# The first feed-forward matmul's last three groups by 26 products of half a batch in place of Strassen's 7, with their weight sums read back from DRAM

## The chip, the core and the metric

The kernel runs on one core of a Trainium2 chip. The core has a matmul engine (TensorE, PE in the profile; its weight loads are shown apart as PEld), three engines that work elementwise on tiles (VectorE = DVE, ScalarE = ACT, GpSimd = POOL) and SyncE (SP), which issues DMAs. Tiles lie in SBUF (128 partitions), matmul results in PSUM, eight banks of 512 float32 a partition. The metric is the device time of one execution in microseconds (us). Before the change it is 1294.29 us, the median of 3 runs (1294.07 to 1294.82).

## The reference

Attention with a root-mean-square norm on q and k, over 8 batches, 12 heads, 448 positions and 64 elements a head, and behind it a feed-forward block with SiLU over all 3584 = 8 x 448 tokens:

```python
q_n, k_n = rmsnorm(q, g_q), rmsnorm(k, g_k)
attn = softmax(scale * q_n @ k_n.T)            # per batch and head
x = (attn @ v).transpose(0, 2, 1, 3).reshape(3584, 768)
h = x @ w_in                                   # w_in  768 x 2048, float64
out = (h * sigmoid(h)) @ w_out                 # w_out 2048 x 768, float64
```

q, k, v are float32. The weights come as float64 and are rounded to float32 in the kernel.

## The kernel before

**Visits.** Four heads at a time make a *visit*, three visits a batch, 24 in all (c = 0 to 23, `NC`). A visit c does the scores and softmax of its heads and the product with v of the visit before (`visit`), with PE's share of attention some 13 us; `between(c)` then does the transposes and fills PE with matmuls of x @ w_in (`fill`). x @ w_in is made for two batches at a time, a *group* of 896 tokens, when their attention is done: group 0 in visits 6 to 11, group 1 in 12 to 17, group 2 in 18 to 23 (`GROUP` = 6), and group 3 alone, after visit 24, with no attention beside it. Then follows the output stage, h @ w_out, for all tokens (`quad`, QUADS = 7), by a deeper Strassen scheme in 192 columns.

**x @ w_in by Strassen.** x lies transposed in SBUF (feature by token, in `sets`). For two tiles of 128 hidden features and the group's two batches, a 2 x 2 scheme needs 7 products in place of 8, each of 3 steps (`HW`) of a 128x128 weight and 448 columns of x. `halves_in` goes through the eight pairs of feature tiles of a group, `part_in` names the operands of a pair, and the class `Seven` does the products: `two` makes products 1 and 2, `five` the others. A product ends in a PSUM bank; ACT copies products 1 and 5 to SBUF, DVE adds the others to what is there (`plus`, L912, one operand in PSUM), POOL adds twice between SBUF tiles (L984, L987). After the pair, ACT applies SiLU and SP writes 128x448 to `hidden` in DRAM (`activate`).

**The sums that Strassen needs.** Of w_in, in four chunks (`room.chunk(i)`, each of four feature tiles, with three sums beside it in `room.sums(i)`), they are made once by DVE (`sum_w_in`) during group 0 and stay in SBUF for all groups. Of x, four DVE operations for each of 3 rows of features make `sums_x` anew for each group (`sum_x`, L909 and L912).

**Rounding.** `Rounder.round` makes one piece of float32 weights of float64 ones: ACT takes two steps, DVE three (L126, L129, L133), POOL one (L137). w_in is rounded in the visits up to 11. w_out is rounded by `prepare_out` beside the products of group 3, two or more pieces at a time, 32 pieces of 128x384, with its Strassen sums by `right_sums` on DVE (L909, 16 of 128x768). It needs 4 chunks of room, which come free in turn: `ORDER` = 3, 0, 1, 2, chunk 3 in the first set of x (`sets[0]`), the others where w_in's chunk of the same number has been used.

**What sets the order.** Each engine works through its instructions in the order in which the program issues them, and waits for semaphores. `fill` issues W_in's matmuls a share at a time, with lists of small jobs (`others`, `prompt`) between them; `weights_in(c, half)` deals out the work on weights to the two halves of a visit. The PSUM banks are dealt by `bank(n)`: in visits one bank "mm" and, at times, one of the scores' ("sc"); once attention is over, two "mm" and six "alone". The other work on DVE in a visit is a merge of softmax parts (L803, 128x896), POOL's are the powers of the norm (L722, L503) and a scaling of q (L731).

## Time and profile before

One execution was profiled. Its span is 1294.6 us, beside the median of 1294.29 us of the three timed runs. The granted clock of PE shows 9, its full digit, in each of the 40 slices.

| engine | busy us | share of span | instructions |
|---|---|---|---|
| PE | 1283.5 | 99% | 7212 |
| PEld | 840.7 | 65% | 7212 |
| DVE | 971.4 | 75% | 1672 |
| ACT | 504.3 | 39% | 880 |
| POOL | 363.5 | 28% | 221 |

The stages, by time: attention alone and group 0 until 311 us, group 1 from 311 to 511, group 2 from 511 to 711, group 3 alone from 711 to 837.7, the output stage from there to the end. The page's slices show where the engines are full; a digit is the busy share of 1/40 of the span (32.4 us) in tenths, and the stage of group 3 are the slices 23 to 26:

```profile
PE   9999999999999999999999999999999999999998
DVE  6898878868666558666555886798978787878785
```

### The profile page before, as it was taken

The numbers are of one execution on the slowest core, as the hardware profiler recorded it, in microseconds if no ns is written. First come the engines' busy times: TensorE is split into PE (matmuls) and PEld (weight loads), VectorE is DVE, ScalarE is ACT, GpSimd is POOL, SyncE is SP. The second block draws the span as 40 slices with busy tenths as digits, with TensorE's granted clock in tenths as the row PEclk, the third lists the DMA queues.
The fourth block names the chain that finished last, engine by engine and source line by source line (L and its number), as shares of the span: only waits on it lengthen the run. The fifth ranks groups of instructions, "written<-read, shape, count | busy, mean of one in ns | idle before, by whom it ended". The sixth has DMA issues, their size and how long they took to land.

```text
span 1294.6 us, 19931 instructions
## 1 busy us (share of the span) xinstructions
PE 1283.5 (99%) x7212; PEld 840.7 (65%) x7212; DVE 971.4 (75%) x1672; ACT 504.3 (39%) x880; POOL 363.5 (28%) x221
## 2 busy tenths in 40 slices
PE   9999999999999999999999999999999999999998
PEld 4444454444444454444544555559999999999998
DVE  6898878868666558666555886798978787878785
ACT  7967666645555554554543344310001000000000
POOL 6765454543344344343311344400000000000000
PEclk9999999999999999999999999999999999999999
DMA  9675347434444444444411466312332313141411
GB/s 232 174 193 136 104 124 197 95 83 102 112 94 91 119 91 102 108 93 93 107 50 69 149 204 219 117 66 88 100 94 86 113 67 129 51 133 48 141 39 40
DMA packets 266160, 144.15 MB, mean 111 GB/s; under 512 B 203748, under 2 KB 249956, under 8 KB 266052
## 3 DMA queue, kind: packets, MB, share of 16 engines
q1 hardware_dynamic: 265424, 141.68, 39.8%
q8 instruction: 59, 0.97, 0.3%
q0 software_dynamic: 320, 0.90, 0.2%
q14 instruction: 49, 0.40, 0.1%
q10 hardware_dynamic: 308, 0.20, 0.1%
HBM read 95.36 MB, written 41.29 MB: 106 GB/s over the span
## 4 chain that ended last, share of the span: by engine, by line
PE 97%; DVE 1%; POOL 1%; issue 0%; ACT 0%; DMA 0%; SPq 0%; ACTq 0%; DVEq 0%; POOLq 0%
PE alone L1285 23%; PE mm L963 21%; PE sc L963 11%; PE av L789 10%; PE sc L752 10%; PE mm L1285 8%; PE alone L963 7%; PE alone L1323 2%; PE mm L832 2%; PE mm L1323 1%; PE sc L643 1%; PE sc L832 1%; PE sc L674 0%; DVE work L912 0%; POOL rms L503 0%
## 5 line engine op out<-in xcount | busy, mean ns | idle before, releaser
L757 ACT ACTIVATE work<-sc,rms 128x448 f32<-128x448 f32 x318 | 182.0, 635 | 98.0 <-PE sc L752 85.7
L752 PE MATMUL sc<-work 64*64 64x448 f32 x1344 | 169.4, 543 | 1.0 <-ACT work L653 0.6
L789 PE MATMUL av<-work,rows 64*64 64x448 f32 x1272 | 155.5, 540 | 1.2 <-DVE x L1514 0.9
L963 PE MATMUL mm<-x,W 128*128 128x448 f32 x366 | 149.1, 542 | 0.0
L963 PE MATMUL mm<-sums_x,W 128*128 128x448 f32 x348 | 142.4, 542 | 0.0
L803 DVE TENSOR_TENSOR work<-work 128x896 f32<-128x896 f32 (+1 forms) x110 | 118.3, 1105 | 28.6 <-PE av L789 28.1
L530 POOL DMA_DIRECT2D out_dram<-x x2 | 1.2, 592 | 443.5 <-DVE x L912 443.5
L503 POOL TENSOR_TENSOR rms<-rms,minus_half 128x14 f32<-128x14 f32 (+4 forms) x40 | 97.4, 2437 | 86.8 <-DVE rms L499 83.3
L963 PEld LDWEIGHTS mm<-x,W 128*128 128x128 f32 x366 | 68.5, 190 | 70.3 <-issue 64.8
L1285 PE MATMUL alone<-W,rows 128*128 128x192 f32 x610 | 113.0, 326 | 0.0
L963 PEld LDWEIGHTS mm<-sums_x,W 128*128 128x128 f32 x348 | 65.1, 190 | 68.1 <-issue 62.5
L789 PEld LDWEIGHTS av<-work,rows 64*64 64x64 f32 x1272 | 65.9, 132 | 62.8 <-issue 19.3
L752 PEld LDWEIGHTS sc<-work 64*64 64x64 f32 x1344 | 60.4, 132 | 63.3 <-ACT work L757 25.3
L1285 PEld LDWEIGHTS alone<-W,rows 128*128 128x128 f32 x610 | 101.4, 190 | 0.0
L963 PE MATMUL sc<-x,W 128*128 128x448 f32 x246 | 99.6, 541 | 0.0
L984 POOL TENSOR_TENSOR stage<-parts,stage 128x448 f32<-128x448 f32 x31 | 39.8, 1285 | 169.2 <-ACT stage L983 168.9
L722 POOL TENSOR_TENSOR rms<-rms,minus_half 128x28 f32<-128x28 f32 x15 | 72.6, 4842 | 48.9 <-DVE rms L719 47.8
L963 PEld LDWEIGHTS sc<-x,W 128*128 128x128 f32 x246 | 46.4, 190 | 47.0 <-issue 46.7
L1285 PE MATMUL alone<-W,work 128*128 128x192 f32 x382 | 72.2, 326 | 0.0
L1295 ACT COPY rows<-alone 128x192 f32<-128x192 f32 x33 | 10.5, 318 | 141.5 <-PE alone L1285 136.7
L1285 PEld LDWEIGHTS alone<-W,work 128*128 128x128 f32 x382 | 63.8, 190 | 0.0
L1116 ACT ACTIVATE stage<-stage 128x896 f32<-128x896 f32 x63 | 56.8, 945 | 17.1 <-DVE stage L912 16.9
(267 smaller groups left out, 2312.8 us busy)
## 6 DMA issues: line engine op xcount, KB each, us to landing
hidden<-stage SPq DMA_DIRECT2D x63, 448.0 KB, 2.9
work<-hidden SPq DMA_DIRECT2D x21, 1024.0 KB, 5.1
rows<-in_moe_w_out_dram SPq DMA_DIRECT2D x32, 384.0 KB, 3.7
W<-in_moe_w_in_dram SPq DMA_DIRECT2D x22, 512.0 KB, 5.3
x<-hidden SPq DMA_DIRECT2D x7, 1024.0 KB, 6.1
rows<-in_q_dram SPq DMA_DIRECT2D x120, 56.0 KB, 2.2
rows<-in_k_dram SPq DMA_DIRECT2D x120, 56.0 KB, 2.3
rows<-in_k_dram SPq DMA_DIRECT2D x60, 96.0 KB, 2.6
```

Of the source, the lines that this page charges most:

```text
L503: nc.gpsimd.tensor_tensor(out=t, in0=t, in1=half, op=ALU.pow)
L722: nc.gpsimd.tensor_tensor(out=f, in0=f, in1=minus_half.to_broadcast([P, n]), op=ALU.pow)
L752: nc.tensor.matmul(two[ds(half * D, D), h, 0:S], keys[rows, ts(half, D)], qT[rows, pair, :], start=True, stop=True,)
L757: nc.scalar.activation(left_weights(c)[:, h] if j == LEFT else weights(c, j)[:, i, h], two[:, h, 0:S], AF.Exp, scale=norm.column(c, i, h, j),)
L789: nc.tensor.matmul(sums[i][ds(h * D, D), :], v, w, start=(j == 0 and step == 1), stop=(j == LEFT - 1 and step == 1),)
L803: nc.vector.tensor_tensor(out=total, in0=total, in1=more, op=ALU.add)
L832: nc.tensor.matmul(t[ds(h * D + i * n, n), :], ones[:, which + i if which else 0], left_weights(c)[:, h] if which else w()[:, i, h], start ...
L963: nc.tensor.matmul(t, self.left(name, s), self.right(name, s), start=s == ends[0], stop=s == ends[1])
L984: nc.gpsimd.tensor_tensor(out=done[1, 2], in0=u2, in1=p5, op=ALU.add)
L1116: nc.scalar.activation(t, t, AF.Silu)
L1285: nc.tensor.matmul(t, x[:, i], y, start=i == ORDER[0], stop=i == ORDER[-1])
L1323: nc.tensor.matmul(o, a[:, 2 * i + m, t], right_one(name, i)[:, m], start=n == 0, stop=n == len(steps) - 1,)
```

## The change

Group 0 stays as it was. For groups 1 to 3, x @ w_in of one chunk (four feature tiles, 512 hidden features) is made by 26 products in place of 28: a scheme of 26 factors for a matrix of 4 by 2 blocks with one of 2 by 4. The blocks of x are half a batch, 224 columns; a product is 3 steps of a 128x128 weight and 224 columns. `FACTORS_LEFT` and `FACTORS_RIGHT` name each product's weight factor and x factor: numbers under 8 are blocks as they are, the others are sums (`LEFT_SUMS` 18 of weights, `RIGHT_SUMS` 18 of x). `AFTER` says which sums of products are made after which product and by which engine (last number: 0 is DVE, 1 POOL), 20 on DVE and 18 on POOL for a chunk.

- **Products** (`products_in`): two products of 224 columns share a PSUM bank; ACT copies the bank into two *blocks* of SBUF (33 blocks of 128x224 in the class `Blocks`, in what were sums of w_in and `stage`). `combine` then does the additions of `AFTER` between blocks, a bank later; when the two halves of a result are ready, ACT applies SiLU in place and SP writes it (`activate_some`).
- **Weight sums** (`form`): one operation of 128x384 each, once per chunk; chunks 0 and 1 on POOL in the visits 7 to 11, chunks 2 and 3 by DVE and POOL in turn in the visits 12 to 15 (`dealt`). `restore` first turns a block of weights that Strassen's sums had overwritten back into itself. `keep` writes each product's weights (128x384) to `lefts` in DRAM in the order of use.
- **Stream** (`Ring`): the weights of two products, 384 KB, are loaded by one DMA from `lefts` into a slot, as soon as a slot is free. There are 3 slots until chunk 2 has been formed (visit 13), 7 after that, 10 while group 3 runs alone, and for its last 13 pairs the 3 slots in the tail of `work`.
- **Sums of x** (`sum_right`): 18 operations of 128x672 a group in place of 12. Four are made a visit early on POOL (`EARLY_SUMS`), 7 on DVE and 7 on POOL in the visits 12 and 18 and ahead of group 3 (`LATE_SUMS`).
- **W_out**: `ORDER` is 0 to 3, the places are `sets[0]`, the room of chunk 3, `work`, the room of chunk 2; `prepare_out` is a flat list of small jobs, of which one is done ahead of each product. The regions of the output stage are dealt anew for that, by `carve` from named areas in place of `take`; what the output stage computes, and in which order, is unchanged.

On DVE, where group 3's products run, the rows read before (W: rooms of weights; stage and parts: results in SBUF; alone and mm: PSUM banks; L126 to L133: rounding of w_out; L909: its sums; L912: Strassen's additions):

```order
L133 SCALAR_TENSOR_TENSOR W<-rows,W 128x384
L909 TENSOR_TENSOR W<-W 128x768 x2
L909 TENSOR_TENSOR W<-W 128x2x384
L909 TENSOR_TENSOR W<-W 128x768
L912 TENSOR_TENSOR parts<-alone,parts 128x448
L912 TENSOR_TENSOR stage<-mm,stage 128x448
L912 TENSOR_TENSOR stage<-alone,parts 128x448
L126 TENSOR_SCALAR W<-W 128x384
L129 TENSOR_SCALAR W<-W 128x384
L133 SCALAR_TENSOR_TENSOR W<-rows,W 128x384
L912 TENSOR_TENSOR stage<-alone,stage 128x448
```

and now (L226 to L233 round, L1009 makes w_out's sums in x_172, which is `sets[0]`, and L1336 is `combine`; W and mixed hold its blocks):

```order
L1009 TENSOR_TENSOR x_172<-x_172 128x768
L226 TENSOR_SCALAR W<-W 128x384
L229 TENSOR_SCALAR W<-W 128x384
L233 SCALAR_TENSOR_TENSOR W<-rows,W 128x384
L1336 TENSOR_TENSOR W<-W 128x224
L1009 TENSOR_TENSOR x_172<-x_172 128x2x384
L1336 TENSOR_TENSOR mixed<-mixed 128x224 x2
L226 TENSOR_SCALAR W<-W 128x384
L229 TENSOR_SCALAR W<-W 128x384
L233 SCALAR_TENSOR_TENSOR W<-rows,W 128x384
L1009 TENSOR_TENSOR x_172<-x_172 128x768
L1336 TENSOR_TENSOR mixed<-mixed,W 128x224
```

The additions of products have half the columns, and none reads a PSUM bank: each has its operands and its result in SBUF.

On POOL at the same place before (L137: last step of rounding; L984 and L987: Strassen's additions):

```order
L137 TENSOR_TENSOR x_172<-x_172,rows 128x384 x2
L137 TENSOR_TENSOR W<-W,rows 128x384 x3
L984 TENSOR_TENSOR stage<-parts,stage 128x448
L137 TENSOR_TENSOR W<-W,rows 128x384
L987 TENSOR_TENSOR stage<-parts,stage 128x448
L137 TENSOR_TENSOR W<-W,rows 128x384 x3
L984 TENSOR_TENSOR stage<-parts,stage 128x448
L137 TENSOR_TENSOR W<-W,rows 128x384
```

and now (L237: last step of rounding; L1336: `combine`):

```order
L1336 TENSOR_TENSOR W<-W 128x224
L237 TENSOR_TENSOR W<-W,rows 128x384
L237 TENSOR_TENSOR W<-W,work 128x384
L1336 TENSOR_TENSOR mixed<-W 128x224
L237 TENSOR_TENSOR W<-W,rows 128x384
L237 TENSOR_TENSOR W<-W,work 128x384
L1336 TENSOR_TENSOR W<-W 128x224 x2
L1336 TENSOR_TENSOR W<-mixed 128x224 x2
L1336 TENSOR_TENSOR W<-W,mixed 128x224 x2
L1336 TENSOR_TENSOR mixed<-mixed 128x224
```

Between the steps of rounding there stand more and shorter additions.

On POOL, where visit 12 begins (group 1), the rows before (L722 and L503: powers of the norm; L731: scaling of q; L984 and L987: Strassen's additions of groups 0 and 1):

```order
L731 TENSOR_TENSOR rows<-rows,rms_61 128x896
L984 TENSOR_TENSOR stage<-parts,stage 128x448
L503 TENSOR_TENSOR rms_60<-rms_60,minus_half 128x14
L987 TENSOR_TENSOR stage<-parts,stage 128x448
L722 TENSOR_TENSOR rms_60<-rms_60,minus_half 128x28
L731 TENSOR_TENSOR rows<-rows,rms_60 128x896
```

and now, from the same scaling of q on (L822, L603 and L831 are the former L722, L503 and L731; L1255: sums of x; L1201: `restore`; L1217: weight sums; L1336: `combine`):

```order
L831 TENSOR_TENSOR rows<-rows,rms_61 128x896
L1255 TENSOR_TENSOR sums_x<-x_173 128x672 x2
L1201 TENSOR_TENSOR W<-W 128x6x128
L1217 TENSOR_TENSOR W<-W 128x384 x2
L1255 TENSOR_TENSOR sums_x<-x_173,sums_x 128x672
L603 TENSOR_TENSOR rms_60<-rms_60,minus_half 128x14
L1217 TENSOR_TENSOR W<-W 128x384
L1336 TENSOR_TENSOR W<-W 128x224
L1217 TENSOR_TENSOR W<-W 128x384
L1255 TENSOR_TENSOR sums_x<-x_173,W 128x672
L1336 TENSOR_TENSOR W<-W 128x224 x2
```

Sums of x and of weights stand ahead of, and between, the powers and additions.

The diff, cut to its core (the tables and the class `Blocks`, which hands out blocks singly or as two that one access reaches, are left out):

```diff
+AFTER = {
+    4: ((16, 100, "-", 104, 0),),
+    6: ((22, 103, "+", 106, 0), (1, 22, "-", 102, 1)),
...
+    def form(i, engines):
+        w = room.chunk(i)
+        s = room.sums(min(i, 3) if i < 2 else 3)
+        tiles = w.rearrange("p (r k f m) -> p r k f m", r=HW, k=2, f=room.CHUNK)
+        slots = [s[:, ds(n * K3, K3)] for n in range(6)]
+        held, order = {}, []
...
+        def restore():
+            halves = w.rearrange("p (c m r k) -> p c m r k", c=z.NW, m=2, r=2)[:, 0:HW]
+            nc.gpsimd.tensor_tensor(
+                out=halves[:, :, :, 1], in0=halves[:, :, :, 0], in1=halves[:, :, :, 1],
+                op=ALU.subtract,
...
+            engines[k % len(engines)].tensor_tensor(
+                out=source(name), in0=a, in1=b, op=ALU.subtract if op == "-" else ALU.add
+            )
+            if k < 4:
+                for n in (2 * k, 2 * k + 1):
+                    keep(n)
+            if order:
+                keep(order.pop())
...
+    def sum_right(group, engine, *names):
+        def one(name):
+            x, op, y = RIGHT_SUMS[name]
+            engine.tensor_tensor(
+                out=right_of(group, name), in0=right_of(group, x), in1=right_of(group, y),
+                op=ALU.subtract if op == "-" else ALU.add,
...
+        def more(self):
+            while self.n < (z.B // 2 - 1) * room.NC * PAIRS:
+                at = self.n % (room.NC * PAIRS)
+                if self.n >= self.last:
+                    self.free = [a for a in self.free if any(a is b for b in self.kept)]
+                if not self.free:
+                    return
+                i, t = divmod(at, PAIRS)
+                assert i in formed
+                slot = self.free.pop(0)
+                nc.sync.dma_start(slot, lefts[i, t])
+                self.ready.append(slot)
+                self.n += 1
...
+    def activate_some(now, most):
+        for _ in range(most):
+            if not silent or silent[0][0] > now:
+                return
+            _, f, b, two = silent.pop(0)
+            t = blocks.two(*two)
+            nc.scalar.activation(t, t, AF.Silu)
+            dst = hidden[f, :, ds(b * S, S)].rearrange("p (two s) -> p two s", two=2)
+            nc.sync.dma_start(dst, t)
+            blocks.release(*two)
...
+                (nc.gpsimd if engine else nc.vector).tensor_tensor(
+                    out=blocks[at[name]], in0=a, in1=b, op=ALU.subtract if op == "-" else ALU.add
+                )
...
+    def products_in(group, beside=lambda: None):
+        last = last_uses()
+        rows = list(carried)
+        carried.clear()
+        for i in range(room.NC):
+            at, places = {}, {}
+            for t in range(PAIRS):
+                slot = stream.next()
+                o = bank(S)
+                for h in range(2):
+                    beside()
+                    b = right_of(group, FACTORS_RIGHT[2 * t + h])
+                    for r in range(HW):
+                        nc.tensor.matmul(
+                            o[:, ts(h, T)], slot[:, ds(h * K3 + r * P, P)], b[:, r],
+                            start=r == 0, stop=r == HW - 1,
+                        )
+                        filler["ended"] = h == 1 and r == HW - 1
+                        yield T
+                filler["ended"] = False
+                now = clock[0] = clock[0] + 1
+                two = blocks.pair()
+                nc.scalar.copy(blocks.two(*two), o.rearrange("p (two s) -> p two s", two=2))
+                at[100 + 2 * t], at[101 + 2 * t] = two
+                stream.done(slot)
+                combine(now)
+                pending.append((at, group, i * room.CHUNK, (2 * t, 2 * t + 1), last, places))
+                if rows and t == 1:
+                    activate(rows)
+                activate_some(now, 2)
+                yield 0
...
-    ORDER = [3, 0, 1, 2]
+    ORDER = list(range(room.NC))
     n1 = room.size1
-    home = {i: (room.chunk(i), room.sums(i)) for i in ORDER[1:]}
-    home[3] = (sets[0][:, ds(0, n1)], sets[0][:, ds(n1, room.size2)])
+    full = n1 + room.size2
+    homes = [sets[0], None, work[:, 0:full], None]
+    home = {
+        i: (a[:, 0:n1], a[:, n1:full]) if a is not None else (room.chunk(j), room.sums(j))
+        for i, a, j in zip(ORDER, homes, (0, 3, 0, 2))
+    }
     bits = ring.bitcast(I32)
+    rows_end = own["rows"][:, 3 * z.DM + z.HALF :]
+    tail = work[:, full:]
...
+    def prepare_out():
+        sums = []
+        for i in ORDER:
+            sums.append([lambda i=i, k=k: right_sums(*chunk_out(i), steps=(k,)) for k in range(4)])
+        work = []
+        for i in ORDER:
+            more = [lambda: None] if not i else sums[i - 1]
+            if i == 2:
+                more = more + [lambda: fetch(0, 1, 1)]
+            for n in range(2 * room.CHUNK):
+                work += [rounder.open, rounder.round]
+                if n < len(more):
+                    work.append(more[n])
+            if i == ORDER[-1]:
+                work += sums[i]
+            while len(work) < (i + 1) * 2 * PAIRS:
+                work.append(lambda: None)
+        return iter(work)
...
+    both = (nc.vector, nc.gpsimd)
+    forms = [
+        form(i, engines) for i, engines in enumerate(((nc.gpsimd,), (nc.gpsimd,), both, both))
+    ]
+    forms[2].append(lambda: (stream.add(room.chunk(2)), stream.more()))
+    dealt = {3: (0, 4), 4: (0, 4), 5: (0, 4), 6: (0, 4), 7: (0, 3)}
+    dealt.update({8: (1, 5), 9: (1, 5), 10: (1, 5), 11: (1, 4)})
+    dealt.update({12: (2, 5), 13: (2, 5), 14: (2, 5), 15: (2, 5)})
+    dealt.update({16: (3, 5), 17: (3, 5), 18: (3, 5), 19: (3, 4)})
...
+    EARLY_SUMS = (11, 16, 12, 24)
+    LATE_SUMS = (8, 14, 22, 10, 15, 21, 17), (19, 9, 13), (18, 25, 23, 20)
...
+        elif c > GROUP and c % GROUP == 0:
+            columns = len(FACTORS_LEFT) * HW * T * room.NC
+            begin(products_in(last_two(c)), columns, 2 * GROUP, T, 2 * HW)
...
+        if c > GROUP and c % GROUP == 0:
+            vector, pool = (
+                sum_right(last_two(c), engine, *names)
+                for engine, names in zip((nc.vector, nc.gpsimd), LATE_SUMS)
+            )
+            run_all(vector[0:2])
+            late = vector[2:6] + late
+            late[2:2] = pool[0:1]
+            late[4:4] = pool[1:2]
+            late += pool[2:] + vector[6:]
...
-    for i in range(HW):
-        sum_x(group, i)
-    for m in range(2):
-        rows = [staged() for _ in range(2)]
-        begun[m] = rows, part_in(group, m, rows)
-        run(begun[m][1].two())
-    run(halves_in(group, range(HF), prepare_out, begun))
+    for engine, names in zip((nc.gpsimd, nc.vector, nc.gpsimd), (LATE_SUMS[i] for i in (1, 0, 2))):
+        run_all(sum_right(group, engine, *names))
+    stream.add(tail[:, 0 : 3 * 2 * K3])
+    stream.kept, stream.last = stream.free[-3:], ((z.B // 2 - 1) * room.NC - 1) * PAIRS
+    asides = prepare_out()
+    run(products_in(group, lambda: next(asides, lambda: None)()))
+    settle()
+    for at in ((0, 0), (0, 1)):
+        fetch(0, *at)
```

287 lines of the change are left out of this document (229 added, 58 removed), and 15 rows, old and new, of tables (AFTER, LEFT_SUMS, RIGHT_SUMS).

## The prediction

> **What bounds the kernel now.** I read the page's busy line and its chain by engine first.
>
> ```profile
> span 1294.6 us, 19931 instructions
> PE 1283.5 (99%) x7212; PEld 840.7 (65%) x7212; DVE 971.4 (75%) x1672; ACT 504.3 (39%) x880; POOL 363.5 (28%) x221
> PE 97%; DVE 1%; POOL 1%; issue 0%; ACT 0%; DMA 0%; SPq 0%; ACTq 0%; DVEq 0%; POOLq 0%
> ```
>
> TensorE is the bound: the chain lies 97% on it. So fewer matmul columns are worth their full time as long as nothing else becomes late. The span of this execution, 1294.6 us, stands 0.3 us above the median of the runs, 1294.29; I work from the span and take 0.3 off at the end.
>
> Next the windows view: two stages that the change rewrites, the second group's first half and the last group, which runs without attention (columns: stretch, length, busy PE, PEld, DVE, ACT, POOL, clock, DMA share, GB/s).
>
> ```profile
> 311.00:411.00 100.00, 99.98 (x548) 49.76 (x548) 66.03 (x89) 52.63 (x82) 40.85 (x18) 1.00 0.43 100
> 711.00:838.00 127.00, 127.00 (x342) 64.32 (x339) 99.28 (x163) 50.55 (x94) 51.76 (x47) 1.00 0.55 178
> ```
>
> In the last group DVE (99 us) and POOL (52 us) add up to more than the 127 us. That matters if the two can't work at once, so I looked for pairs that overlap in the timelines of both engines.
>
> ```profile
> 272.83 1.13 POOL L984 TENSOR_TENSOR stage<-parts,stage 128x448 f32<-128x448 f32 x1 [3.00 <-ACT stage L983]
> 388.77 1.91 POOL L987 TENSOR_TENSOR stage<-parts,stage 128x448 f32<-128x448 f32 x1 [6.28 <-DVE parts L912]
> 388.61 1.07 DVE L803 TENSOR_TENSOR work<-work 128x896 f32<-128x896 f32 x1
> 389.70 0.62 DVE L912 TENSOR_TENSOR stage<-sc,stage 128x448 f32<-128x448 f32 x1
> 259.35 1.91 POOL L987 TENSOR_TENSOR stage<-parts,stage 128x448 f32<-128x448 f32 x1 [0.18 <-DVE parts L912]
> 260.19 1.89 DVE L912 TENSOR_TENSOR W<-W 128x768 f32<-128x768 f32 x1
> 310.94 4.79 POOL L722 TENSOR_TENSOR rms<-rms,minus_half 128x28 f32<-128x28 f32 x1 [2.90 <-DVE rms L719]
> 314.56 0.62 DVE L909 TENSOR_TENSOR sums_x<-x,sums_x 128x448 f32<-128x448 f32 x1
> ```
>
> A POOL add of 448 columns takes 1.13 us alone, but 1.91 when a DVE add of two SBUF tiles (L803, from 388.61) is under way. A DVE add of two SBUF tiles that starts inside a POOL add (260.19, inside 259.35 to 261.26) takes 1.89, and its group below has a mean of 0.99: it waited out POOL's 1.07. A DVE add with one operand in PSUM (389.70, sc) ends inside the POOL add at its usual 0.62. So POOL's tile operations and DVE's operations on SBUF operands alone exclude each other; I call that the **port**. POOL's power on rms (L722, 310.94 to 315.73) is not part of it: DVE's add at 314.56 keeps its 0.62.
>
> **TensorE: what goes.** The chain gives back-to-back pitches for three widths.
>
> ```profile
> 711.18 2.45 PE mm L963 x6
> 713.63 6.76 PE alone L963 x18
> 837.66 5.16 PE mm L1323 x16
> 842.82 15.48 PE alone L1323 x48
> 880.24 3.90 PE alone L1285 x24
> ```
>
> 448 columns: 6.76/18 = 375.6 ns; 384: 15.48/48 = 322.5; 192: 3.90/24 = 162.5. The last two give 0.833 ns a column and 2.5 ns for each record, and 448 lies on that line, so 224 columns take 189.2 ns. A group before is 8 x 7 products x 3 steps at two records each, 336 x 375.7 = 126.2 us (711.18 to 837.66 is 126.5). After, it is 4 chunks x 26 products x 3 x 2 = 624 records x 189.2 = 118.1. That is **8.2 us a group, 24.5 us for three**; visits 12 to 23 get 1.4 us each shorter. No trace row has 224 columns: from below it can't beat 186.7 ns (0.833 x 224), which is 1.6 us more a group; from above it can't exceed the 322.5 of the 384.
>
> [...]
>
> **The port in the last group: what comes.** Prices first.
>
> ```profile
> L803 DVE TENSOR_TENSOR work<-work 128x896 f32<-128x896 f32 x78 | 84.3, 1114 | 28.1 <-PE av L789 28.1
> L909 DVE TENSOR_TENSOR W<-W 128x768 f32<-128x768 f32 x24 | 23.0, 992 | 2.7 <-POOL W L137 2.7
> L912 DVE TENSOR_TENSOR work<-work,x 128x384 f32<-128x384 f32 x28 | 15.5, 555 | 0.5
> 842.25 3.68 DVE L909 TENSOR_TENSOR W<-W 128x192 f32<-128x192 f32 x12
> 779.37 1.00 POOL L137 TENSOR_TENSOR W<-W,rows 128x384 int32<-128x384 int32 x1 [2.08 <-DVE W L133]
> 781.75 0.99 POOL L137 TENSOR_TENSOR W<-W,rows 128x384 int32<-128x384 int32 x1 [1.38 <-DVE W L133]
> 133.03 1.28 POOL L137 TENSOR_TENSOR W<-W 128x512 int32<-128x512 int32 x1 [1.56 <-DVE W L133]
> ```
>
> POOL: 384 columns 0.99, 448 1.13, 512 1.28, so 2.3 ns a column: 224 takes 0.615 us, 672 1.66. DVE: twelve adds of 192 in 3.68, 0.307 each; 32 columns more at 1.14 ns (768 against 384) make 0.34 for 224, and 672 takes 0.8. One rounded piece of W_out costs 2.37 us of the port (POOL's adds at 779.37 and 781.75: three DVE steps of 1.38 together, then POOL's 0.99, never side by side). In the last group after the change:
> - combinations (AFTER: per chunk 20 on DVE, 18 on POOL, every operand in SBUF): 80 x 0.34 = 27 and 72 x 0.615 = 44. Before, DVE's 40 adds read PSUM and cost the port nothing; POOL's 16 cost 18.
> - rounding, unchanged: 32 x 2.37 = 76. W_out's sums, unchanged: 16 x 0.9 = 14.
> - sums of x: 7 on DVE, 7 on POOL, 5.5 + 11.6 = 17. Before: 12 on DVE, 6.5.
>
> Sum 178 us, against 115 before (18 + 76 + 14 + 6.5), which fitted into 126. How much of the sum is really spent shows in the busiest stretch of before:
>
> ```profile
> 723.23 0.35 DVE L126 TENSOR_SCALAR x<-x 128x384 f32<-128x384 f32 x1
> 732.35 0.56 DVE L133 SCALAR_TENSOR_TENSOR x<-rows,x 128x384 int32<-128x384 int32 x1
> 724.74 1.00 POOL L137 TENSOR_TENSOR x<-x,rows 128x384 int32<-128x384 int32 x1 [19.13 <-DVE x L133]
> 730.70 1.00 POOL L137 TENSOR_TENSOR x<-x,rows 128x384 int32<-128x384 int32 x1 [0.98 <-DVE x L133]
> ```
>
> From 723.23 to 732.91, 9.7 us, stand four DVE roundings and five POOL adds (three of 384, two of 448 between the two quoted): by my prices 4 x 1.38 + 3 x 0.99 + 2 x 1.13 = 10.8. So 0.9 of the sum: **161 us**, more than TensorE's 118. Bounds: 118 if all overlapped (each engine alone has under 92), 179 if nothing does. I take 161, nearest to that stretch. TensorE can't run away from it: its products end in 8 banks, which ACT empties into blocks that the combinations free, and the output's first product needs W_out's last sum.
>
> ```profile
> 712.32 0.62 DVE L909 TENSOR_TENSOR sums_x<-x 128x448 f32<-128x448 f32 x1
> 836.04 2.69 DVE L909 TENSOR_TENSOR W<-W 128x768 f32<-128x768 f32 x3 [0.89 <-POOL W L137]
> ```
>
> Before, the port's work runs from 712.3 to 838.7 and the output stage starts at 837.7.
>
> **Visits 12 and 18** carry the sums of x, and 12 and 13 the weight sums of chunk 2. A visit:
>
> ```profile
> 344.78 0.16 DVE L765 COPY av<-minus_half 128x1 f32<-128x1 f32 x1 [0.69 <-PE av L789]
> 377.97 0.16 DVE L765 COPY av<-minus_half 128x1 f32<-128x1 f32 x1 [0.67 <-PE av L789]
> L731 POOL TENSOR_TENSOR rows<-rows,rms 128x896 f32<-128x896 f32 x12 | 21.0, 1748 | 0.9
> ```
>
> 33.2 us, 31.8 after. Port in visit 12: POOL 7 x 1.66 (x) + 4 x 0.99 and a restore of 768 at 1.9 (weights) + 12 x 0.615 + 1.75 (L731) = 26.6; DVE 4.6 x 1.1 (L803) + 7 x 0.8 + 5 x 0.55 + 13 x 0.34 = 17.8. Together 44, so 13 over; visit 13 has 26 and catches up. Visit 18, without weight sums: 36, 4 over. Of these 17 us between none and all reach TensorE; I take **7**, since 13 us of the next visit are attention and leave the port room.
>
> [...]
>
> **Hidden edits.** The weights now come from DRAM: 384 KB a pair of products, which TensorE uses for 12 x 189.2 = 2.27 us.
>
> ```profile
> rows<-in_moe_w_out_dram SPq DMA_DIRECT2D x32, 384.0 KB, 3.7
> 335.41 3.98 SPq L255 DMA_DIRECT2D rows<-in_k_dram  x8
> ```
>
> The ring has three slots in visits 12 and 13 and for the last 13 pairs: a load has two pairs, 4.5 us, and takes 3.7 by the row of the same size. I cost it at nothing; cover is gone when SP is busy with eight loads of k (3.98 us), which would cost 3.2 us each time. ACT gains 13 copies a chunk and stays under 60%. The first group's POOL sums (36 in five visits) lie in its idle time. W_out's new places and the output stage move no work. Three 1 MB fetches now start when the products end, about 10 us ahead of need: nothing.
>
> **Sum.** Groups two and three: -16.4 + 7 = -9.4, so the last group's port work starts at 702.9 and ends at 702.9 + 161 = 863.9. The output starts 1.5 us ahead of that end (the last combinations follow W_out's sum), at 862.4 in place of 837.7: +24.7. 1294.6 + 24.7 - 0.3 = 1319, which I round to **1320**.
>
> **Rivals.**
> - DVE and POOL fit into each other's gaps at this small size, and TensorE stays the bound. Then 1294.3 - 24.5 + 7 = **1277**, faster. For it: each engine alone has time; against it: rows 260.19 and 388.77. It decides below a port time of 136 us (837.7 + 1.5 - 702.9), where the result turns from slower to faster.
> - Port time between 136 and 150: 1294 to 1308, about the same to slower.
> - The weight stream is late as well: SP stands behind k's loads twice in visits 12 and 13 and its waits for POOL's sums come on top, 4 x 3.2 = 13 us on 1320, **1333**.
> - The change doesn't do what it says: 224 columns at more than 202 ns (126.2/624) save nothing. The records' own mean, 326 ns at 192 columns unpipelined, would be its extreme; the pitch rows speak against it. Some 1345.
>
> **How the numbers follow.** Forecast 0.58; overlap (1277) 0.20; between 0.12; late stream 0.08; no saving 0.02. The range reaches from the overlap's 1276 to 1338 (port 179). Faster by over 0.2%, about what a measurement of this kernel can tell from no change: the overlap and a fifth of the between, 0.22; within 0.2%: 0.05; slower: 0.73. On the slower side alone the range is 1300 to 1338.
>
> **What would show it.** Right: in the last group gaps of TensorE that end on ACT or on DVE's and POOL's adds, DVE and POOL adds well over 0.34 and 0.615 us in the mean, that group some 160 us long. Wrong: TensorE without gaps there and L1371 at 189 ns, or its waits ending on loads of lefts.

## The result, and the profile after

The changed kernel takes 1433.39 us, the median of 4 runs (1431.76 to 1438.17), beside 1294.18 (1293.99 to 1294.82, 4 runs) for the kernel before: 1.108 times as long (95% interval 1.106 to 1.110), 139 us slower. The page's first lines, and of its 40 slices those of TensorE and its granted clock:

```profile
span 1431.5 us, 22959 instructions
PE 1302.4 (91%) x8076; PEld 1018.8 (71%) x8076; DVE 1080.7 (75%) x1795; ACT 561.8 (39%) x1036; POOL 604.5 (42%) x480
PE   9999989997758799898999799488999999999997
PEclk9999999998979899999999999799999999999999
```

TensorE is no longer full, and in four of the slices in which it isn't (10, 12, 14 and 26) its granted clock shows 8, 7, 8 and 7 in place of 9. To see in which stage, I cut the span at the visits (DVE's copy of av<-minus_half stands at the head of each visit from 7 on) and at the output's first matmul: the visits 7 to 11, 12 to 15, 16 to 23, group 3 and the output stage. Before:

```profile
149.70:311.30 161.60, 161.60 (x907) 80.13 (x903) 125.89 (x172) 96.43 (x153) 70.92 (x40) 1.00 0.50 124
311.30:444.50 133.20, 133.16 (x724) 66.15 (x720) 86.34 (x116) 71.48 (x111) 52.34 (x23) 1.00 0.44 104
444.50:710.00 265.50, 265.37 (x1424) 130.08 (x1416) 168.23 (x223) 133.30 (x208) 90.71 (x42) 1.00 0.35 87
710.00:837.70 127.70, 127.50 (x345) 64.35 (x346) 99.12 (x163) 50.61 (x95) 51.76 (x47) 1.00 0.55 178
837.70:1294.60 456.90, 450.74 (x2648) 433.50 (x2646) 365.21 (x806) 39.86 (x112) 3.38 (x5) 1.00 0.26 85
```

and after:

```profile
149.30:330.80 181.50, 166.90 (x903) 79.86 (x895) 135.56 (x170) 96.55 (x153) 118.48 (x81) 0.98 0.63 168
330.80:522.00 191.20, 146.01 (x918) 110.61 (x920) 108.28 (x152) 81.70 (x140) 104.95 (x80) 0.87 0.67 193
522.00:801.20 279.20, 259.58 (x1808) 202.40 (x1800) 208.71 (x278) 159.21 (x279) 170.91 (x136) 0.98 0.69 187
801.20:964.00 162.80, 131.33 (x633) 125.16 (x634) 131.00 (x193) 69.14 (x143) 103.53 (x106) 0.90 0.70 238
964.00:1431.50 467.50, 453.67 (x2649) 434.58 (x2647) 371.07 (x813) 42.79 (x119) 9.88 (x14) 0.99 0.28 89
```

The columns are stretch, length, busy PE, PEld, DVE, ACT and POOL, clock, DMA share and GB/s. Length less busy PE is TensorE's idle time. The saving of matmul time is 8.2 us a group, so 5.5 us in four visits and 10.9 in eight; what busy PE has above its time before less this saving is time in which matmuls ran slowly, most of it at half clock, as is shown below.

| stage | before | after | saved | idle more | slow matmuls |
|---|---|---|---|---|---|
| visits 7 to 11 | 161.6 | 181.5 | 0 | 14.6 | 5.3 |
| visits 12 to 15 | 133.2 | 191.2 | 5.5 | 45.2 | 18.3 |
| visits 16 to 23 | 265.5 | 279.2 | 10.9 | 19.5 | 5.1 |
| group 3 | 127.7 | 162.8 | 8.2 | 31.3 | 12.0 |
| output stage | 456.9 | 467.5 | 0 | 7.7 | 2.9 |

So 24.6 us were saved, and 118 us of waits and 44 us of slow matmuls came. The saving itself is there. In TensorE's timeline, in group 3, twelve matmuls of 224 columns follow each other in 2.27 us, 189.2 ns each:

```profile
809.78 2.43 PE L1371 MATMUL alone<-x,W 128*128 128x224 f32 x12
812.05 2.43 PE L1371 MATMUL alone<-W 128*128 128x224 f32 x12
814.32 2.43 PE L1371 MATMUL mm<-x,W 128*128 128x224 f32 x12
...
370.61 6.34 PE L1371 MATMUL mm<-sums_x,W 128*128 128x224 f32 x24 [2.55 <-DMA W<-lefts]
...
896.35 1.37 PE L1371 MATMUL alone<-sums_x,W 128*128 128x224 f32 x6 [2.12 <-ACT work L204]
...
920.73 2.58 PE L1371 MATMUL alone<-W,work 128*128 128x224 f32 x6 [14.42 <-DMA work<-lefts]
923.10 2.45 PE L1371 MATMUL alone<-x,work 128*128 128x224 f32 x6
925.34 1.99 PE L1371 MATMUL mm<-x,work 128*128 128x224 f32 x6
927.17 1.30 PE L1371 MATMUL mm<-W,work 128*128 128x224 f32 x6
```

The last rows show the slow matmuls: after an idle time of 14.42 us, six take 2.37 us from start to start (920.73 to 923.10), twice their 1.14, and it takes 6 us until they are back. After 2.12 us of idle time nothing of it is seen; after 2.55 it is (24 in 6.34 us, where 24 at 189.2 ns take 4.5). In this trace every wait from 3.7 us on has it, and none under 2 us. The trace's record of the granted clock has 17 stretches at half clock up to the last matmul, each of 3.41 us or two, three or five times that. The length of a wait alone doesn't tell whether one comes: waits of 2.02, 2.23, 2.29, 2.55 and 3.07 us brought the half clock, and 2.12 and 3.38 us didn't. The 17 stretches are 109 us long, and TensorE was busy in 72 us of them; half of that, 36 us, is the clock's part of the 44. The other 8 us are not placed.

TensorE's longest waits in all:

```profile
PE mm L1371 <- DMA W<-lefts: 27.3, 9, 6.5
PE alone L1371 <- DMA work<-lefts: 24.4, 3, 14.4
PE mm L1371 <- DVE W L1336: 8.9, 1, 8.9
```

(us in total, times, longest.) The weight stream leads, with nearly half of the 118 us. Where its loads were, SP's timeline tells; first visit 12, then group 3:

```profile
345.49 3.98 SPq L355 DMA_DIRECT2D rows<-in_q_dram  x8
349.59 0.40 SPq L1285 DMA_DIRECT2D W<-lefts  x1
350.10 1.09 SPq L1104 DMA_DIRECT2D hidden<-mixed  x2
351.24 5.05 SPq L1197 DMA_DIRECT2D lefts<-W  x6
356.39 0.51 SPq L1285 DMA_DIRECT2D W<-lefts  x1
...
801.25 20.15 SPq L188 DMA_DIRECT2D rows<-in_moe_w_out_dram  x4
821.50 1.32 SPq L1285 DMA_DIRECT2D work<-lefts  x3
...
909.34 7.56 SPq L188 DMA_DIRECT2D rows<-in_moe_w_out_dram  x3
916.95 0.42 SPq L1285 DMA_DIRECT2D work<-lefts  x1
```

A load of the stream (L1285) stands behind eight loads of q, behind six writes of weight sums (L1197, 0.84 us each in the mean), or behind loads of w_out (L188) that wait for a buffer which rounding has yet to free: 801.25 to 821.4. SP's own waits in group 3 begin with these two (us in total, times, longest; L233 is DVE's last step of rounding):

```profile
SPq L188 <- DVE W L233: 27.7, 11, 4.6
SPq L188 <- DVE x L233: 27.4, 5, 18.1
```

### The profile page after: what moved, and what is told of

Read it like the earlier page. It is cut to its first block, busy times and chain, and to the rows that moved or that the text cites. A ratio compares the mean times of both kernels' runs of the same rounds, so it can differ in the third digit from the quotient of the medians.

```text
span 1431.5 us, 22959 instructions
## 1 busy us (share of the span) xinstructions
PE 1302.4 (91%) x8076; PEld 1018.8 (71%) x8076; DVE 1080.7 (75%) x1795; ACT 561.8 (39%) x1036; POOL 604.5 (42%) x480
## 5 line engine op out<-in xcount | busy, mean ns | idle before, releaser
L603 POOL TENSOR_TENSOR rms<-rms,minus_half 128x14 f32<-128x14 f32 (+4 forms) x40 | 101.1, 2530 | 71.8 <-DVE rms L599 68.7
L1629 PE MATMUL alone<-W,x 128*128 128x192 f32 x544 | 112.6, 326 | 0.0
L1629 PEld LDWEIGHTS alone<-W,x 128*128 128x128 f32 x544 | 92.5, 190 | 0.0
L1371 PE MATMUL mm<-W 128*128 128x224 f32 x306 | 72.2, 381 | 20.8 <-DMA W<-lefts 11.7
L822 POOL TENSOR_TENSOR rms<-rms,minus_half 128x28 f32<-128x28 f32 x15 | 72.4, 4825 | 40.4 <-DVE rms L819 39.6
L1371 PE MATMUL mm<-x,W 128*128 128x224 f32 x312 | 73.8, 375 | 15.2 <-DMA W<-lefts 13.0
L1371 PEld LDWEIGHTS mm<-W 128*128 128x128 f32 x306 | 62.2, 207 | 25.6 <-DVE W L1336 9.2
L1217 POOL TENSOR_TENSOR W<-W 128x384 f32<-128x384 f32 x54 | 60.5, 1136 | 25.9 <-DVE W L1217 18.1
L1639 ACT COPY sums_x<-alone 128x192 f32<-128x192 f32 x33 | 10.5, 318 | 141.0 <-PE alone L1629 141.0
L1065 PE MATMUL mm<-x,W 128*128 128x448 f32 x138 | 56.7, 546 | 3.4 <-ACT mixed L1076 1.7
L1643 ACT COPY x<-alone 128x192 f32<-128x192 f32 x34 | 10.9, 319 | 123.0 <-PE alone L1629 114.2
L1629 PE MATMUL alone<-W,work 128*128 128x192 f32 x244 | 57.2, 326 | 0.0
L1012 DVE TENSOR_TENSOR rows<-rows,x 128x192 f32<-128x192 f32 x72 | 25.7, 357 | 38.2 <-ACT x L1643 36.4
L575 DVE TENSOR_REDUCE rms<-rows 128x8 f32<-128x512 f32 (+2 forms) x50 | 31.9, 639 | 26.3 <-ACT rows L574 25.8
```

Of the source, the lines that this page charges most:

```text
L575: nc.vector.tensor_reduce(out=out, in_=t.rearrange("p (n d) -> p n d", n=n), axis=AX.X, op=ALU.add)
L603: nc.gpsimd.tensor_tensor(out=t, in0=t, in1=half, op=ALU.pow)
L822: nc.gpsimd.tensor_tensor(out=f, in0=f, in1=minus_half.to_broadcast([P, n]), op=ALU.pow)
L1012: nc.vector.tensor_tensor(out=out, in0=a, in1=b, op=ALU.add)
L1065: nc.tensor.matmul(t, self.left(name, s), self.right(name, s), start=s == ends[0], stop=s == ends[1])
L1217: engines[k % len(engines)].tensor_tensor(out=source(name), in0=a, in1=b, op=ALU.subtract if op == "-" else ALU.add)
```

## The experiments

Each kernel is the change with the edits shown; "as e2" and the like say whose edits it has besides. This table has the lengths of the stages, read as above; the output stage is counted to its last matmul. The column "whole" is the time of the run or, for the change, for e1 and e15, a median. A kernel that leaves work out can't be compared as a whole, only by stages. The lengths are those of one execution each, and they differ between runs whose edits don't concern the stage: 177.6 (e2) to 184.2 us (e9) for the visits 7 to 11, 191.0 to 193.6 (e9, e10) for 12 to 15, 278.7 to 282.2 (e10, e4) for 16 to 23, 160.3 to 162.9 (e3, e2) for group 3. So a difference of a few us between two runs, up to 6.6 in the visits 7 to 11, shows nothing by itself.

| run | whole | 7 to 11 | 12 to 15 | 16 to 23 | group 3 | output |
|---|---|---|---|---|---|---|
| before | 1294.2 | 161.6 | 133.2 | 265.5 | 127.5 | 450.9 |
| the change | 1433.4 | 181.5 | 191.2 | 279.2 | 162.8 | 459.2 |
| e1 ACT issues the loads | 1419.0 | 181.0 | 180.4 | 285.5 | 157.1 | 457.4 |
| e2 no sums, no writes, chunks 2, 3 | 1406.1 | 177.6 | 168.5 | 280.1 | 162.9 | 459.3 |
| e3 no writes, chunks 2, 3 | 1410.4 | 181.2 | 171.1 | 279.5 | 160.3 | 459.9 |
| e4 no sums, chunks 0, 1 | 1420.8 | 167.8 | 191.3 | 282.2 | 162.3 | 459.9 |
| e5 as e2, ACT issues the loads | 1384.1 | 180.2 | 149.6 | 284.7 | 156.7 | 457.3 |
| e6 as e2, seven slots | 1378.0 | 182.2 | 138.3 | 280.5 | 161.5 | 460.0 |
| e7 as e1, all product sums on DVE | 1404.5 | 179.0 | 189.3 | 276.8 | 150.6 | 453.0 |
| e8 no sums of x | 1398.6 | 175.8 | 188.9 | 265.4 | 150.9 | 459.9 |
| e9 less rounding of w_out | 1410.1 | 184.2 | 191.0 | 279.9 | 141.5 | 457.1 |
| e10 no loads for the last 13 pairs | 1421.6 | 181.1 | 193.6 | 278.7 | 135.5 | 476.1 |
| e11 every new addition on DVE | 1417.3 | 196.5 | 188.6 | 280.1 | 137.2 | 459.2 |
| e12 half the bytes of the stream | 1414.5 | 179.5 | 184.1 | 278.2 | 155.4 | 459.3 |
| e13 as e6, no sums of x | 1344.7 | 175.7 | 135.9 | 266.9 | 151.1 | 459.6 |
| e14 no sums, no writes, chunks 0, 1 | 1411.0 | 164.3 | 186.2 | 283.4 | 162.6 | 459.3 |
| e15 as e7, slots freed earlier | 1404.0 | 180.3 | 194.8 | 274.8 | 141.0 | 457.6 |

Two theories stood against each other: the *queue theory* (the stream's loads are issued late, behind the other work in SP's queue, as from 801.25 to 821.4 us, and three slots don't cover that) and the *port theory* of the prediction (DVE and POOL exclude each other on SBUF, as it read its rows 260.19 and 388.77, so sums and blocks are late).

**e1: the loads on ACT's queue.**

```diff
-                nc.sync.dma_start(slot, lefts[i, t])
+                nc.scalar.dma_start(slot, lefts[i, t])
```

> The loads of the weight stream are issued by ACT in place of SP; nothing else changes. Queue theory: TensorE's waits for lefts (24 us in the visits 12 to 14, 25 us beside group 3) come from loads that stand in SP's queue behind the writes of weight sums, the loads of q, k, v and the loads of w_out that wait for rounding. Then these waits go, with some 10 us of half-clock matmuls behind them: 1370 to 1395 in place of 1433, group 3 near 135 us. Port theory (DVE and POOL exclude each other, sums and blocks are late): other waits take their place, group 3 stays at 155 or more, 1420 to 1433.

1418.99 us, above the queue theory's range and just under the port's. The visits 12 to 15 gain 11 us and group 3 only 5.7: of the waits for lefts in group 3 9.7 us are left, but 14.6 us of waits for ACT's SiLU (behind blocks that DVE and POOL finish) came in their place. The visits 16 to 23 got 6.3 us longer.

**e2 and e3: chunks 2 and 3 without sums and writes, and without writes alone.**

```diff
+    forms[2], forms[3] = [lambda: None] * 19, [lambda: None] * 19   # e2
-                if name == n:
+                if name == n and i < 2:                              # e3
-                nc.sync.dma_start(slot, lefts[i, t])
+                nc.sync.dma_start(slot, lefts[i % 2, t])             # both
```

> The weight sums of chunks 2 and 3 and their writes to DRAM are left out (their products load the weights of chunks 0 and 1 instead). Both theories: the visits 12 to 15 (191 us now, 133 before the change) fall to about 130 us, the whole by some 60 us to 1375. If they stay above 150, the stream itself or the sums of x are to blame.

> The weight sums of chunks 2 and 3 are made, but not written to DRAM (their products load the weights of chunks 0 and 1). Queue theory: SP has 9 to 11 us less to issue in each of the visits 12 to 15, and nothing waits for a write: the four visits fall from 191 to 140 to 150 us. Port theory: the 36 additions are what costs; the four visits stay above 175 us.

Without the writes the four visits take 171.1 us, without writes and sums 168.5. So the 52 writes cost 20 us; the 2.6 of the 36 additions are within what runs differ by. The port theory, which said 175 or more without the writes, falls for this place. What it is in a write that costs, these runs don't separate. Beside SP's time, DVE stood idle in the four visits until a write had landed and the place of its sum could be used again:

```profile
DVE W L1217 <- DMA lefts<-W: 19.5, 6, 7.2
```

e3 takes away both, SP's work and this wait. But 168.5 is far above the 130 that both expected: visits 12 and 13 still take 46.6 and 57.6 us, 14 and 15 are down to 32.6 and 31.7. What the first two have alone is three slots and the late sums of x.

**e5 and e6: the same without SP, and with seven slots.** (e6 has SP issue the loads.)

```diff
+                nc.scalar.dma_start(slot, lefts[i % 2, t])           # e5
                 stream.add(room.sums(2))
+                stream.add(room.chunk(2))                            # e6
```

> The weight sums of chunks 2 and 3 and their writes are left out (their products load chunks 0 and 1), and ACT issues the stream's loads; three slots in the visits 12 and 13. Queue theory: with SP's queue out of the way the stream is on time, the visits 12 and 13 take 34 us each (46.6 and 57.6 with the loads on SP). Slot theory: a slot comes free two pairs, 4.5 us, ahead of its next use, and a load takes 4.6 us from issue to landing; the waits for lefts stay, at 40 us or more a visit.

> As the run without the sums of chunks 2 and 3, with SP issuing the loads, but with seven slots from visit 12 on in place of three. Slot theory: the visits 12 and 13 fall from 46.6 and 57.6 to 34 us each, since a load may be six pairs late. Queue theory: SP's eight loads of q or k (4 us) are covered by seven slots as well, so the same. If they stay above 40 us, neither slots nor SP's queue are it, but the sums of x on DVE and POOL.

The visits 12 to 15 in e2, e5 and e6 (columns as above):

```profile
327.15:495.63 168.48, 141.78 (x918) 110.89 (x920) 94.19 (x133) 81.30 (x140) 79.91 (x60) 0.90 0.59 162
327.45:477.09 149.64, 135.97 (x918) 102.84 (x920) 93.49 (x134) 81.84 (x140) 79.08 (x60) 0.96 0.69 183
329.44:467.77 138.33, 133.44 (x918) 103.40 (x920) 92.03 (x134) 81.17 (x140) 80.46 (x60) 0.96 0.73 199
```

With three slots and ACT's queue visits 12 and 13 take 42.0 and 43.0 us, with seven slots 34.6 and 39.5, and no wait for lefts is left in the four visits. Of the 30 us that four more slots bring (168.5 to 138.3), 19 come by the queue alone (149.6). So it is slots and queue together: three slots were too few for loads that were issued late. (All three runs are without weight sums and writes; whether seven slots would have covered the writes too, no run shows.)

**e12: half the bytes.**

```diff
-                nc.sync.dma_start(slot, lefts[i, t])
+                nc.sync.dma_start(slot[:, 0:K3], lefts[i, t, :, 0:K3])
-                            o[:, ts(h, T)], slot[:, ds(h * K3 + r * P, P)], b[:, r],
+                            o[:, ts(h, T)], slot[:, ds(r * P, P)], b[:, r],
```

> Each load of the weight stream brings 192 KB in place of 384 (both products of a pair use the first one's weights); number, order and slots stay. Transfer theory: the 4.6 to 5.5 us from issue to landing are transfer time on busy DMA engines and fall to some 3.5; with three slots and 4.5 us that ends the waits for lefts where SP isn't late: the visits 12 and 13 fall from 112 to about 90, group 3 by 10. Queue theory: the issue itself is late, not the transfer; the visits and group 3 change by less than 5 us.

Landing fell as the transfer theory said. The DMA view of the stretch from 330 to 490 us, the change and then e12 (count, KB each, median us from issue to landing):

```profile
W<-lefts SPq DMA_DIRECT2D x31, 384.0 KB, 4.2
```

```profile
W<-lefts SPq DMA_DIRECT2D x29, 192.0 KB, 3.2
```

One microsecond less, and visits 12 and 13 fell only from 112.0 to 107.8 us, where the transfer theory said 90; group 3 fell by 7.4. So in the visits late issue weighed more than the transfer.

**e4, e14 and e11: the weight sums of chunks 0 and 1 in the visits 7 to 11.** e4 leaves the sums out, e14 the writes too (its products load other data from DRAM); e11 moves all additions that the change brought, these among them, from POOL to DVE; as in e15, ACT issues the loads and a slot is freed by its own pair, so e11 is to be compared with e15.

```diff
+            if i > 1:                                                # e4
                 engines[k % len(engines)].tensor_tensor(
...
+    forms[0], forms[1] = [lambda: None] * 19, [lambda: None] * 19   # e14
...
-        form(i, engines) for i, engines in enumerate(((nc.gpsimd,), (nc.gpsimd,), both, both))
+        form(i, engines) for i, engines in enumerate(((nc.vector,),) * 4)    # e11
...
-            engine.tensor_tensor(
+            nc.vector.tensor_tensor(                                 # e11
```

> The 36 weight sums of chunks 0 and 1 on POOL (visits 7 to 11) are left out; their writes to DRAM stay. Port theory: the five visits, 181.5 us now against 161.6 before the change, come back to 162 to 166 us. Queue theory (52 writes on SP): they stay above 176 us.

> The weight sums of chunks 0 and 1 and their writes are left out (their products load other data of the same size from DRAM). If the writes are the 6 us that stayed without the sums, the visits 7 to 11 take 161 to 164 us (167.8 without the sums alone, 161.6 before the change). Rival, the sums of x of visit 11 and other moves: 166 or more.

> All additions on POOL that the change brought are made by DVE (products' sums, sums of x, weight sums of all chunks), ACT issues the loads, and a slot is handed on as soon as its own products are done. Port theory: POOL's tile operations cost the port 1.8 times DVE's; the visits 7 to 11 come from 181 to 172 us, 16 to 23 from 277 to 268, group 3 from 151 to 138, the whole from 1404 to about 1375. Rival, DVE alone becomes the bound in the visits: 7 to 11 above 181.

181.5 us became 167.8 without the sums, 13.7 of the 19.9 us that were lost. The 3.5 that go with the writes (164.3) and the 2.7 that are left are within what runs differ by. The port has a part in it: on nearly the same instructions (170 and 172) DVE was busy for 135.6 us in these visits, 125.9 before, and 127.8 in e4 without POOL's sums. But e11 went against the port theory: with the engine that the theory prices lower the five visits got longer, 196.5 us beside 180.3 in e15, where 172 was expected. There, TensorE waits for Strassen's additions on DVE (mixed L1012, 17.4 us in all, against 3.7 in the change). So it isn't the port's sum alone that counts there: I read the waits so that DVE's additions empty TensorE's banks, and what stands ahead of them in DVE's queue delays TensorE. Group 3 of e11, 137.2 us, came out as the port theory said (138); the visits 16 to 23 (280.1 for 268) and the whole (1417.3 for 1375) didn't.

**e8 and e13: no sums of x,** alone and on top of e6.

```diff
-        return [lambda name=name: one(name) for name in names]
+        return [lambda: None for name in names]
```

> All 18 sums of x of the three last groups are left out. Port theory: the visits 17 to 19, 111 us now, come to 100; visit 23 from 35.9 to 33; group 3 starts its rounding 15 us earlier and ends 10 to 15 us earlier (162.8 to 150); the visits 12 to 15 fall by 10 at most, since their loads of weights are late anyway. Rival, the sums of x lie beside other work: no stage changes by more than 4 us.

> As the run with seven slots and without the weight sums of chunks 2 and 3, and the sums of x are left out too. If slots, writes, weight sums and sums of x are the whole loss, the visits 12 to 15 take 4 x 31.9 = 127 to 130 us (138.3 with the sums of x) and 16 to 23 take 262 to 266. Rival, the 26 products' own additions and copies delay TensorE too: 134 or more in the first four.

Without them the visits 16 to 23 lose 13.8 us, the visits 7 to 11 5.7 (visit 11, which makes four sums ahead, falls from 37.2 to 32.9), group 3 11.9. Visits 17 to 19 fall from 111.3 to 101.2. In e13 the visits 12 to 15 take 135.9 us, where the rival said 134 or more: against 127.7 (before less saving) 8 us stay:

```profile
323.03:458.92 135.89, 130.20 (x918) 102.36 (x912) 85.22 (x126) 81.29 (x140) 66.56 (x53) 0.99 0.78 206
```

5.7 of them are idle time, and TensorE's waits there end on ACT's copies of the products (3.1 us) and on loads of the stream (2.4). So the products' own copies and additions may delay TensorE too; no run took these away.

**e7, e9 and e10: what holds group 3.** e7 has e1's edit and gives all 38 additions a chunk to DVE; e9 leaves out two DVE steps and POOL's step of each rounding of w_out; e10 leaves out the last 13 loads.

```diff
-                (nc.gpsimd if engine else nc.vector).tensor_tensor(
+                nc.vector.tensor_tensor(                             # e7
...
+    rounder.short = True      # e9: L226, L229 and L237 are skipped
...
+                if self.n < self.last:                               # e10
                     nc.sync.dma_start(slot, lefts[i, t])
```

> ACT issues the loads, and all 38 additions a chunk of the products are made by DVE (18 were POOL's). Port theory: the sum that DVE and POOL may not overlap falls by 72 x (0.615 - 0.34) = 20 us for group 3, which goes from 157 to about 140; the visits 16 to 23 from 285 to 270 to 280. Rival, DVE alone is the bound there: group 3 gets longer, 165 or more.

> Of the rounding of w_out beside group 3 only DVE's last step stays; two DVE steps and POOL's addition of each of the 32 pieces are left out (32 x 1.7 = 55 us of the port). Loads, their order on SP and their buffers stay. Port theory: the port's sum falls from 161 to 111 us, under TensorE's 118, and group 3, 162.8 us long, comes to 130 to 135. Queue and slot theory alone: its last 13 pairs wait for their weights as before, 150 or more.

> The loads of the weight stream for the last 13 pairs of group 3 (three slots, behind the loads of w_out on SP) are left out; the products use what lies in the slots. Queue and slot theory: TensorE's 20 us of waits for these loads and some 6 us of half-clock matmuls behind them go, group 3 comes from 162.8 to about 137. Port theory: rounding and additions end when they did, waits for ACT, DVE or POOL take the place, 150 or more.

In e10 the products end 135.5 us after the group's begin, as the queue theory said (about 137), and then the output stage waits. Its TensorE and DVE rows, and in the third fence the last sums of w_out in the change:

```profile
958.34 2.29 PE L1668 MATMUL mm<-W,rows 128*128 128x384 f32 x3 [16.65 <-DVE W L1009]
```

```profile
956.01 2.27 DVE L1009 TENSOR_TENSOR W<-W 128x768 f32<-128x768 f32 x2
```

```profile
965.90 2.28 DVE L1009 TENSOR_TENSOR W<-W 128x768 f32<-128x768 f32 x2
```

The last sum of w_out ends at 958.3, 156 us after the group's begin at 802.1, and in the change at 968.2, 167 us after 801.2. So without the late loads rounding and additions would still have held the output stage back, and the whole gained 12 us, not 27. e9 and e7 bear out the port theory only in part. e9, with 55 us of port work less, took 21 us off the group: 141.5, between the port's 130 to 135 and the queue's 150 or more. It doesn't separate the two either, since less rounding frees w_out's buffers and with them SP's queue sooner: the waits for loads of lefts fell from 25.6 to 14.7 us. e7 came to 150.6, 6.5 less than e1, where the port theory said about 140 and its rival 165 or more. The exclusion itself shows at the begin of group 3 in the change, where a sum of x on DVE that begins ahead of POOL's takes 0.85 us, and the next one, beside POOL's, 2.15:

```profile
804.37 0.85 DVE L1255 TENSOR_TENSOR W<-x 128x672 f32<-128x672 f32 x1
805.25 2.15 DVE L1255 TENSOR_TENSOR W<-x,W 128x672 f32<-128x672 f32 x1
804.60 4.28 POOL L1255 TENSOR_TENSOR sums_x<-x 128x672 f32<-128x672 f32 x2 [2.21 <-DVE x L963]
```

The groups of DVE's additions show it too, over the whole run, in the change and then in e7, where POOL makes none of them (busy, mean ns):

```profile
L1336 DVE TENSOR_TENSOR W<-W 128x224 f32<-128x224 f32 x59 | 33.2, 570 | 17.1 <-ACT W L1380 14.5 <-POOL mixed L1336 1.5
L1336 DVE TENSOR_TENSOR mixed<-mixed,W 128x224 f32<-128x224 f32 x52 | 34.4, 671 | 7.8 <-ACT mixed L1380 5.6 <-POOL W L1336 1.3 <-POOL mixed L1336 0.2
```

```profile
L1336 DVE TENSOR_TENSOR W<-W 128x224 f32<-128x224 f32 x89 | 40.0, 460 | 10.3 <-ACT W L1380 9.3
L1336 DVE TENSOR_TENSOR mixed<-mixed,W 128x224 f32<-128x224 f32 x88 | 39.8, 463 | 0.7
```

**e15: the whole computation with what helped.** A slot is freed by its own pair, not by the next:

```diff
-            if self.used is not None:
-                self.free.append(self.used)
-            self.used = slot
+            self.free.append(slot)
```

> The whole computation: ACT issues the loads, a slot is handed on as soon as its own products are done, and DVE makes all additions of products; sums of x and of weights stay on POOL and DVE as in the change. Both theories: group 3 near 140 us (150.6 with a slot held a pair longer), the visits as in that run, 1390 to 1400; still slower than 1294.

1403.98 us, 1.084 times the time before (1.081 to 1.087), and just above the 1390 to 1400 that was expected. Group 3 came to 141.0, as expected, but the visits 12 to 15 to 194.8, with 31.8 us of waits for ACT's copies (TensorE's longest wait there, and then one of ACT's own):

```profile
PE mm L932 <- ACT mixed L1378: 31.8, 3, 12.9
```

```profile
ACT work L792 <- DMA lefts<-W: 14.6, 1, 14.6
```

ACT, which now issues the loads too, stood 14.6 us until a write of weights had landed. So the queue's delay moved with the loads; what part of the 31.8 us it makes, no run shows. No complete version that was run beats the kernel before.

## Why the prediction was wrong

- **TensorE's saving: right.** 189.2 ns a record, as worked out from the three other widths.
- **"Hidden edits", the weight stream: wrong, and the largest miss.** The step was "The ring has three slots in visits 12 and 13 ... I cost it at nothing". The visits 12 to 15 lost 63.5 us against 127.7. Taken away one after the other, the weight sums and their writes make 23 of them (20 the writes, e3), three slots in place of seven 30 (e2 to e6), 19 of these by SP's queue (e5), and the sums of x 2 (e13, within what runs differ by); 8 stay. I saw k's loads ahead of the stream, and in a rival the writes' waits for POOL, but did not count the writes themselves: 52 more on the same queue, 0.32 to 1.22 us each, and DVE's waits for their landing. The landing time was taken from another load's row, 3.7 us, and came out at 4.2 in the stretch from 330 to 490 us; half the bytes took only 7.1 us off the four visits (e12). The rival of the late stream had the mechanism, at 13 us.
- **"The first group's POOL sums ... lie in its idle time": wrong.** The sums cost 13.7 of the 19.9 us that the visits 7 to 11 lost (e4). POOL had the time, but its sums held up DVE, by some 8 us of busy time (135.6 beside 127.8); that this reaches TensorE by way of DVE's emptying of the banks is my reading of the waits, and not shown by a run.
- **Visits 12 and 18, "I take 7": mis-sized.** The stalls fall also in the visits that make the next group's sums (11, 17, 23) and in 19. The visits 16 to 23 lost 24.6 us against 254.6, of which 13.8 go with the sums of x (e8); the other 10.8 are not placed.
- **The port in the last group: right in size, but not by the path that was named.** 161 us were worked out; from the first sum of x (804.4) to the end of w_out's last (968.2) it took 163.8, and in e10 some 153. DVE's additions of 128x224 took 0.54 to 0.73 us in the mean of their groups there and POOL's 0.73 to 0.86, over 0.34 and 0.615 as the prediction asked. But it also said that waits of TensorE that end on loads of lefts would show it wrong, and 25.6 of the 36.3 us of waits in group 3 do. What wasn't seen is that rounding, late by the port as I read it, held w_out's loads on SP (L188 waited 27.7 and 27.4 us for L233) and through them the stream. Since the port's work would have ended late anyway, these loads cost 12 us (e10). That the group's 162.8 us lie so near to 161 is in part luck: two delays overlap in it.
- **The end of the sum: wrong by the start.** "The last group's port work starts at 702.9": its first sum of x starts at 804.4, 101.5 us later, and there nearly all of the 112 us of error lies; the output stage, which took 10.6 longer, has the rest.
- **The fetches, "about 10 us ahead of need: nothing": wrong.** The output stage waits 5.3 us for x<-hidden, and its matmuls take 2.9 us more than before.
- **Not in the prediction: the clock.** Before, TensorE had no gap of more than 0.3 us after the first visits (from 80 us on), so its trace had no row of what follows a gap. 44 us of the loss are slow matmuls, 36 of them by the half clock behind waits.

## What to carry to other kernels

A transfer that is "hidden" must be followed through its issuing queue: list everything that stands ahead of it there, with issue times and with what each of these waits for, then count the buffers against that delay (here loads of w_out for 20.15 us ahead of three of the stream), not against the landing time alone (4.2 us in the median from 330 to 490 us). An engine with idle time is no free place for new work when its work holds up the engine that frees TensorE's banks, as POOL's sums did with DVE in the visits 7 to 11 (135.6 us busy, 127.8 without them); ask whose result TensorE waits for next, and what the new work puts ahead of it. And price a stall of a full TensorE higher than its length: here 118 us of waits came with 44 us of slow matmuls.

## What the runs showed of the hardware

- In the changed kernel's trace TensorE ran at half clock behind every wait from 3.7 us on, behind five waits of 2.02 to 3.07 us and not behind two of 2.12 and 3.38, and behind none under 2. The half clock came in stretches of 3.41 us or a multiple of it, up to 17.1.
- The 104 writes of 192 KB of weights held SP for 0.32 to 1.22 us each, 0.48 in the median (six in a row 5.05), a load of 384 KB of the stream for 0.40 and 0.51 beside them.
- DVE's sum of 128x224 took 448 to 463 ns in the mean of its four largest groups with the products' additions off POOL (e7), and 570 to 671 with them on it (the change).
- POOL's power (L722, L503) left DVE's additions as they were: in the trace before, 32 of 128x448 between SBUF tiles that lie wholly inside one took 0.56 to 0.63 us, 0.62 in the median, as the other 48 did in the median (0.62).
